# Attention head and mixture chain on one core: a new start for the first pair, and q's scaling moved within the attention loop

## The chip, the cores and the metric

The kernel runs on one core of a Trainium2 chip. The metric is the time of one execution on the device in microseconds (us); lower is better. Five engines work in parallel, each through its own instructions in order: TensorE (PE: matmuls, and PEld for its weight loads), VectorE (DVE), ScalarE (ACT), GpSimd (POOL) and SyncE (SP, which only issues DMAs). They wait for each other on semaphores. ACT and POOL can issue DMAs too.

## The reference

Three stages follow each other: an attention in which a query sees only the keys of its own hash bucket, and two feed-forward layers.

```python
q_bits = einsum('bhsd,dk->bhsk', q, proj) > 0      # 6 bits for each row; k the same
mask = bucket(q_bits)[..., :, None] == bucket(k_bits)[..., None, :]
scores = where(mask, q @ k.T / sqrt(64), -1e9)      # B=2, H=8, S=768, D=64
attn = softmax(scores);  x = attn @ v               # then reshaped to 1536 x 512
x = relu(x @ w_in)**2 @ w_out                       # d_ff 2048
out = silu(x @ w_in2) @ w_out2
```

Everything is float32; the weights arrive as float64 words and are converted on the chip.

## The kernel before

Attention treats two heads at a time, a pair: eight pairs, of four units each (a head's 384 queries), of three blocks of 128 queries. One pass of the loop over `d` is a step: it takes one block of scores through reduce and exp, transposes two key blocks of an earlier unit, splits them in a high and a low part and multiplies them with v. A float32 product is made from float32r parts, high times high, high times low and low times high; so q (`qq`), k (`kk`), the transposed P (`th`, `tl`) and v exist as high and low parts. The mask is made inside the product: bits of q and k stand as twelve more rows of `qq[:, 1]` and `kk[:, 1]`, so the scores need four matmuls.

What a step issues, by engine:
- DVE: `row_max` (a reduce of 768 scores, L699), two small `row_live` operations (L703, L704), two `t_lo` (the low part `tl`, L738).
- ACT: two `t_hi` (L732), `score_exp` (L712).
- PE: six transposes (L727), four matmuls with v (L751, L752), four of scores (L694).

Seven steps (d = 5, 17, 29, ... 77) are in the dictionary `long`. In them PE also makes the bits of the next pair (twelve matmuls, L525), DVE compares them (`bits_cmp`, L531, twice), and from d = 17 on PE transposes the reciprocal sums of the pair before (`rb_mm`, L776), which ACT copies (`x_norm`, L786). Then ACT issues a DMA (L618) that places bits of k. Five of them (d = 5, 17, 29, 53, 65) and the one at 77 also hold operations on VectorE that convert feed-forward weights (`w_exp` L657, `w_sign` L661, `w_low` L665), in the list `mid`.

The next pair but one is prepared meanwhile: q is loaded, ScalarE scales it in place by 1/8 (`scale_q`, L494), POOL casts it (`cast_pair`, tile hq, L490), and later steps split and place it. `scale_q` stands at the end of the step ahead of a long one.

The head, d = -5 to 1, does the first pair by other functions. Its second head's rows of k come by a DMA of POOL (`second_head`, L591). `first_bits_mm` (L605) makes the bits of q and of k separately, for each head and half, as 76 columns of which the last twelve are the bits, and `first_bits_cmp` (L609) writes them straight into `qq` and `kk`. `warm_up` issues matmuls on zeros.

The order of each engine is the order in which the program is written; in the feed-forward part, which the change leaves alone, a planner with costs sets it. A PSUM tile of the scores has two buffers, so a block's scores wait until the exp of the block two before has read them.

Of the kernel before, what the change touches and what calls it, by code (L numbers as in the profile page):

```python
# [11 lines left out]
F32 = mybir.dt.float32  # L12
# [11 lines left out]
NB = 6  # L24
# [5 lines left out]
NBR = 2 * NB  # L30
NFQ = 3 * NBR + 6
PW = 96
# [403 lines left out]
def lsh_attention_moe_moe(ctx, tc, kd, qk, qf, fq, v, pc, wi1, wo1, wi2, wo2, out):  # L436
# [25 lines left out]
    pcr = ac.tile([128, 2 * PW], F32, name="pcr")  # L462
    tmt = ac.tile([128, 6], F32, name="tmt")
# [3 lines left out]
    pjd = ac.tile([128, 3, 76], F32R, name="pjd")  # L467
    pdx = ac.tile([128, 2, NBR], F32, name="pdx")
    tm = [tmt[:, 2 * i : 2 * i + 2] for i in range(3)]
    mt = ac.tile([128, 4, 4], F32, name="mt")  # L470
# [75 lines left out]
    def first_load(h):  # L546
# [11 lines left out]
        else:  # L558
            first[1, 0] = a1.tile([128, S], F32, tag="tb", name="fr10")
            first[1, 1] = a1.tile([128, 6, 2, 64], F32, tag="rw", name="fr11").rearrange("p a b c -> p (a b c)")  # L560
            for i in range(2):
                nc.sync.dma_start(out=first[1, i], in_=qf[1, i])
        t["qq"][h] = a1.tile([128, 2, S], F32R, tag="qq", bufs=2, name=f"qq0_{h}")
        t["kk"][h] = a1.tile([128, 2, S], F32R, tag="kk", bufs=2, name=f"kk0_{h}")
        first["hk", h] = (a2 if h else a1).tile([128, S], F32R, tag=("hk", "hq")[h], name=f"hk0_{h}")

    def first_q_hi(z):
        nc.scalar.mul(out=pair[0]["qq"][0][:, 0, half(z)], in_=first[0, 0][z], mul=SCALE)

    def first_q_lo(z):  # L570
        qq = pair[0]["qq"][0]
        nc.vector.scalar_tensor_tensor(
            out=qq[0:64, 1, half(z)], in0=first[0, 0][z][0:64], scalar=SCALE, in1=qq[0:64, 0, half(z)].bitcast(F32), op0=ALU.mult, op1=ALU.subtract
        )

    def first_k_hi(z):
        for i in range(2):
            nc.scalar.copy(out=pair[0]["kk"][0][0:64, i, half(z)], in_=first[0, 1][z][0:64])

    def first_k_lo(z):  # L580
        r, hk = first[0, 1][z], first["hk", 0]
        if z == 0:
            nc.gpsimd.tensor_copy(out=hk[64:128, half(z)], in_=r[64:128])
        else:
            nc.scalar.copy(out=hk[64:128, half(z)], in_=r[64:128])
        nc.gpsimd.tensor_tensor(out=pair[0]["kk"][0][64:128, 0, half(z)], in0=r[64:128], in1=hk[64:128, half(z)].bitcast(F32), op=ALU.subtract)
# [12 lines left out]
    def first_bits_mm(h, i, z):  # L599
        x, zs = pair[0][("qq", "kk")[i]][h], half(z)  # L600
        o = first["bits", h, i, z] = ps_t.tile([128, 512], F32, tag="t", name=f"bf{h}{i}{z}")
        w = (pjd[:, i], x[:, 0, zs]), (pjd[0:64, 2 * i], x[0:64, 1, zs])
        for n in range(2):
            wt_, xt = w[n ^ i]
            mm(o[0:76, 0:QW], wt_, xt, start=n == 0, stop=n == 1)  # L605

    def first_bits_cmp(h, i, z):
        m = tm[1 + i][64:76]
        nc.vector.tensor_scalar(  # L609
            out=pair[0][("qq", "kk")[i]][h][64:76, 1, half(z)], in0=first["bits", h, i, z][64:76, 0:QW],  # L610
            scalar1=m[:, 0:1], scalar2=m[:, 1:2], op0=ALU.is_gt, op1=ALU.mult,
        )

    def place_bits(p, h):
# [200 lines left out]
    mid = defaultdict(list)  # L815
    long = {}
    last = defaultdict(list)
# [53 lines left out]
    with tc.manual_schedule():  # L871
# [19 lines left out]
        nc.vector.tensor_copy(out=pjd.rearrange("p a b -> p (a b)"), in_=zero[:, 0:228])  # L891
        c, k = slice(64, 64 + NBR), first["c"]
# [8 lines left out]
        nc.vector.tensor_tensor(out=pjd[0:64, 2, c], in0=pdx[0:64, 1], in1=pjd[0:64, 1, c].bitcast(F32), op=ALU.subtract)
        first_k_lo(0)
        first_k_hi(0)
        first_k_lo(1)
        first_k_hi(1)
        first_q_hi(1)
        for i, z in ((0, 0), (1, 0), (1, 1)):
            first_bits_mm(0, i, z)
        for i, z in ((0, 0), (1, 0), (1, 1)):
            first_bits_cmp(0, i, z)  # L910
        first_q_lo(1)
        at(-4, first_bits_mm, 0, 0, 1)
        mid[-3].append((first_bits_cmp, (0, 0, 1)))
        for n, (i, z) in enumerate(((1, 0), (1, 1), (0, 0), (0, 1))):
            at((-3, -3, -2, -1)[n], first_bits_mm, 1, i, z)
            mid[n - 2].append((first_bits_cmp, (1, i, z)))
        second_head()
# [13 lines left out]
        for d in range(-5, G // 2 + 3):  # L931
# [52 lines left out]
        assert not new  # L984
        assert not todo and not extra and not mid
        att.close()
# [18 lines left out]
def _layout(q, k, v, proj, moe_w_in, moe_w_out, moe2_w_in, moe2_w_out):  # L1005
# [43 lines left out]
```

## Time and profile before

| what | us |
|---|---|
| median of 3 runs (758.18 to 759.3) | 758.25 |
| the profiled execution | 754.1 |
| its span | 752.3 |
| PE busy in the span | 737.8 (98%) |
| DVE busy | 596.6 (79%) |
| ACT busy | 460.3 (61%) |
| POOL busy | 427.6 (57%) |

The span is the part of the profiled execution between its first and last instruction. A busy PE is not a PE at its peak, since matmuls are pipelined. The granted clock of TensorE is 1.00 (2.4 GHz) or 0.50 (1.2 GHz) of full speed; its mean over the span is 0.997.

### The profile page before, as it was taken

The page shows a single profiled execution, that of the slowest core. Times are in us where ns is not written, and L with a number is a line of the kernel's source. Part 1 is how long each engine was busy: PE and PEld are TensorE (multiplying, and loading weights), DVE is VectorE, ACT ScalarE, POOL GpSimd, SP SyncE. Part 2 cuts the span into 40 slices and gives each one's busy share as a digit, 9 for nine tenths or more (in the row PEclk, how much of TensorE's full clock was granted, in tenths as well). Part 3 has the DMA queues.
Part 4 walks back from the last instruction along what each step waited for, and adds up shares of the span by engine and source line. Part 5 has one row for each costly group of instructions (what it writes and reads, how often), then busy time and mean ns, then how long its engine had stood idle before and what let it go on. Part 6 is the DMA issues. An engine that isn't in the chain of part 4 may idle for free.

```text
span 752.3 us, 10873 instructions
## 1 busy us (share of the span) xinstructions
PE 737.8 (98%) x3732; PEld 629.0 (84%) x3732; DVE 596.6 (79%) x1053; ACT 460.3 (61%) x865; POOL 427.6 (57%) x316
## 2 busy tenths in 40 slices
PE   8899999999999999999999999999999999999998
PEld 3789999999998778888888888887888888888886
DVE  6899999999999898659558786999965874685542
ACT  5788989998898774575368258447534525624510
POOL 7457497578591567654655743967475356455200
PEclk9999999999999999999999999999999999999999
DMA  7566866776642312122221221102122121030012
GB/s 229 117 144 153 210 162 167 178 161 146 152 103 88 95 57 84 57 84 61 81 84 57 85 84 58 53 32 85 57 84 85 48 93 55 31 112 29 0 71 98
DMA packets 27654, 71.98 MB, mean 96 GB/s; under 512 B 4192, under 2 KB 9072, under 8 KB 27600
## 3 DMA queue, kind: packets, MB, share of 16 engines
q1 hardware_dynamic: 24936, 64.64, 30.2%
q0 software_dynamic: 2208, 6.00, 3.6%
q10 hardware_dynamic: 456, 0.65, 0.4%
q8 instruction: 30, 0.49, 0.3%
q14 instruction: 24, 0.20, 0.1%
HBM read 49.80 MB, written 3.15 MB: 70 GB/s over the span
## 4 chain that ended last, share of the span: by engine, by line
PE 69%; DVE 27%; DMA 1%; issue 1%; ACT 1%; POOL 0%; ACTq 0%; DVEq 0%
PE bank L338 33%; PE bank L257 17%; PE bank L228 9%; DVE mt L699 8%; DVE tl L738 8%; PE s L694 4%; PE t L727 3%; DVE ys L151 2%; PE o L751 2%; PE o L752 1%; DVE xb L157 1%; DMA kk<-in_dram 1%; DVE mt L704 1%; DVE ts L262 1%; DVE wt L174 1%
## 5 line engine op out<-in xcount | busy, mean ns | idle before, releaser
L172 POOL TENSOR_SCALAR wt<-wt 128x512 f32<-128x512 f32 x56 | 117.0, 2098 | 45.3 <-ACT wt L170 45.3
L157 POOL TENSOR_TENSOR wp<-wt,wp 128x512 fp32r<-128x512 f32 x56 | 76.6, 1378 | 96.1 <-ACT wp L155 96.1
L257 PE MATMUL bank<-xb,wp 128*128 128x512 f32 x480 | 111.3, 390 | 2.8 <-DVE ts L262 1.6
L257 PEld LDWEIGHTS bank<-xb,wp 128*128 128x128 f32 x480 | 89.7, 188 | 23.0 <-DVE xb L157 1.6
L738 DVE TENSOR_TENSOR tl<-t,th 128x384 fp32r<-128x384 f32 x192 | 104.8, 547 | 3.3 <-ACT th L732 2.7
L712 ACT ACTIVATE P<-s,mt 128x768 f32<-128x768 f32 x96 | 95.7, 997 | 14.7 <-DVE mt L704 11.8
L155 ACT CAST wp<-wt 128x512 fp32r<-128x512 f32 x56 | 34.6, 620 | 105.7 <-DVE wt L175 64.4
L699 DVE TENSOR_REDUCE mt<-s 128x1 f32<-128x768 f32 x96 | 91.4, 952 | 5.3 <-PE s L694 4.7
L732 ACT CAST th<-t 128x384 fp32r<-128x384 f32 x192 | 82.4, 484 | 13.1 <-PE t L727 9.9
L694 PE MATMUL s<-kk,qq 76*128 76x384 f32 (+1 forms) x384 | 85.1, 342 | 1.3 <-ACT P L712 0.5
L727 PE MATMUL t<-ident,P 128*128 128x128 f32 x576 | 80.8, 275 | 4.5 <-DVE tl L738 3.1
L262 DVE TENSOR_TENSOR ts<-bank,ts 128x512 f32<-128x512 f32 x80 | 54.6, 690 | 36.7 <-PE bank L257 34.4
L228 PE MATMUL bank<-x0h,wp 128*128 128x512 f32 x256 | 80.2, 390 | 0.0
L727 PEld LDWEIGHTS t<-ident,P 128*128 128x128 f32 x576 | 68.5, 141 | 10.5 <-issue 3.9
L751 PE MATMUL o<-th,vv 128*128 128x384 f32 x192 | 72.9, 380 | 0.0
L694 PEld LDWEIGHTS s<-kk,qq 76*128 76x128 f32 (+1 forms) x384 | 68.1, 190 | 3.8 <-DVE bt L531 1.8
L752 PE MATMUL o<-tl,vv 128*128 128x384 f32 x192 | 64.5, 336 | 0.0
L242 ACT ACTIVATE ts<-bank 128x512 f32<-128x512 f32 x48 | 28.6, 595 | 52.4 <-PE bank L228 26.9
L228 PEld LDWEIGHTS bank<-x0h,wp 128*128 128x128 f32 x256 | 48.1, 188 | 9.9
L157 DVE TENSOR_TENSOR gql<-ts,gqh 128x512 fp32r<-128x512 f32 x64 | 46.1, 732 | 12.7 <-ACT gqh L155 12.4
L174 DVE SCALAR_TENSOR_TENSOR wt<-raw,wt 128x512 uint32<-128x512 uint32 x58 | 51.5, 889 | 0.6
L170 ACT ACTIVATE wt<-raw 128x512 f32<-128x512 f32 x58 | 38.7, 670 | 20.5 <-POOL wp L157 11.0
(169 smaller groups left out, 1725.7 us busy)
## 6 DMA issues: line engine op xcount, KB each, us to landing
raw<-in_dram SPq DMA_DIRECT2D x64, 512.0 KB
kk<-in_dram POOLq DMA_DIRECT2D x15, 384.0 KB, 5.3
qq<-hq SPq DMA_DIRECT2D x28, 192.0 KB
vr<-in_dram SPq DMA_DIRECT2D x8, 384.0 KB
ta<-ob SPq DMA_DIRECT2D x32, 96.0 KB
tb<-ob SPq DMA_DIRECT2D x32, 96.0 KB
out_dram<-ts SPq DMA_DIRECT2D x11, 256.0 KB
rq<-in_dram SPq DMA_DIRECT2D x7, 384.0 KB
```

The source lines that it names most:

```text
L157: add(("DVE", "POOL")[pool], l, lambda: eng.tensor_tensor(out=lo(), in0=src(), in1=hi().bitcast(F32), op=ALU.subtract), (*rk, *hk), lk)
L172: add("DVE" if fast else "POOL", 0.5 if fast else 2.4, lambda: eng.tensor_scalar(out=wtt, in0=wtt, scalar1=W_LO, scalar2=W_HI, op0=ALU.max ...
L228: mm(bank[b], w[:, x, op, sl], t["x0"][y][:, kt], start=kt == 0 and j == 0, stop=kt == 3 and j == 2)
L257: mm(bank[b], w[:, p, op, k * 128 : k * 128 + 128], x[:, q, xop, k], start=first and k == 0 and j == 0, stop=k == 1 and j == 2, skip_group ...
L338: mm(bank[b][:, 0:wd], x, y, start=i == 0 and n == 0, stop=i == FB - 1 and n == 2)
L694: mm(s[:, n, 0:QW], t["qq"][h][0:kk, ab, c0 : c0 + 128], t["kk"][h][0:kk, ab, n * QW : (n + 1) * QW], start=ab == 0, stop=ab == 1)
L699: nc.vector.tensor_reduce(out=m[:, 0:1], in_=s[:, :, 0:QW], op=ALU.max, axis=AX.XY, negate=True)
L712: nc.scalar.activation(out=e.rearrange("p (a b) -> p a b", a=2), in_=s[:, :, 0:QW], func=AF.Exp, scale=m[:, 1:2], bias=m[:, 2:3], accum_ou ...
L727: nc.tensor.transpose(t[:, j * 128 : (j + 1) * 128], P[u, j][:, kt * 128 : (kt + 1) * 128], ident)
L732: nc.scalar.copy(out=th, in_=PT[g][0][:, 0:QW])
L738: nc.vector.tensor_tensor(out=tl, in0=t[:, 0:QW], in1=th.bitcast(F32), op=ALU.subtract)
L751: mm(o[:, 0:QW], vv, th, start=kt == 0, stop=False)
```

## The change

Four things are done.
- In the attention loop, `scale_q` of pairs 2 to 7 moves from the end of the step ahead of a long step into the long step, behind its `score_exp`.
- In the head, low parts are made by POOL instead of VectorE in part, the first head's bits of k are made from three operands (the high part of k twice, from `hk`), and the DMA with the second head's rows of k is issued by POOL before the splits. The DMA of `pcr` goes to ACT's queue.
- The second head's bits of q and k are made together as 24 columns, two groups of four matmuls instead of four groups of two; they are compared into a tile `bt`, and two DMAs on ACT's queue place them (`second_place`).
- The warm-ups follow a table: 9 instead of 12 at the start, one between groups of bits, and 3, 2, 3, 3, 3, 2, 1 in steps -5 to 1 (before: 2 in steps -5 to -2). Loads of weights 0 and 1 are written at step -2 instead of -5, `scale_q` of pair 1 at -3 instead of -1, and the load of pair 2 at 1 instead of -1.

```diff
+WARM = {-5: 3, -4: 2, -3: 3, -2: 3, -1: 3, 0: 2, 1: 1}
-W_STEPS = ((-5, 2, 5, 5, 17), (-5, 5, 17, 29, 29), ...
+W_STEPS = ((-2, 2, 5, 5, 17), (-2, 5, 17, 29, 29), ...
...
+            nc.scalar.dma_start(out=pcr, in_=pc)
...
     def first_q_lo(z):
+        q, qq = first[0, 0][z][0:64], pair[0]["qq"][0]
+        if z:
+            nc.gpsimd.tensor_tensor(out=qq[0:64, 1, half(z)], in0=q, in1=qq[0:64, 0, half(z)].bitcast(F32), op=ALU.subtract)
+        else:
+            nc.vector.scalar_tensor_tensor(...)
+    def first_k_hi(z, i):
+        (nc.gpsimd.tensor_copy if i else nc.scalar.copy)(out=pair[0]["kk"][0][0:64, i, half(z)], in_=first[0, 1][z][0:64])
+    def first_hk(z):
+        nc.scalar.copy(out=first["hk", 0][64:128, half(z)], in_=first[0, 1][z][64:128])
+    def first_k_lo(z):
+        (nc.gpsimd if z else nc.vector).tensor_tensor(...)
...
+    def second_bits_mm(z):
+        o = first["both", z] = ps_t.tile([128, 512], F32, tag="t", name=f"bs{z}")
+        ops = [(64 - NBR * i, *x) for i in range(2) for x in first_ops(1, z)[i]]
+        for n, (c, w, rows_, x) in enumerate(ops):
+            mm(o[0 : 2 * NBR, 0:QW], pjd[rows_, w, c : c + 2 * NBR], x, start=n == 0, stop=n == len(ops) - 1)
+    def second_bits_cmp(z):
+        ...
+        nc.vector.tensor_scalar(out=first["bt"][0 : 2 * NBR, half(z)], in0=first["both", z][0 : 2 * NBR, 0:QW], ...)
+    def second_place():
+        for n, x in enumerate(("qq", "kk")):
+            nc.scalar.dma_start(out=pair[0][x][1][64 : 64 + NBR, 1, :].bitcast(F32), in_=first["bt"][NBR * n : NBR * n + NBR].bitcast(F32))
...
-            at(d0 - 13, load_pair, p)
-            at(d0 - 8, scale_q, p)
+            at(max(d0 - 13, 1), load_pair, p)
+            scale[d0 - 7] = p
...
-        warm_up(12)
+        warm_up(9)
+        nc.gpsimd.dma_start(out=pair[0]["kk"][1][0:64], in_=kd[0, :, 1].unsqueeze(1).broadcast_to([64, 2, S]))
...
+        for z in range(2):
+            at(z - 2, second_bits_mm, z)
+            mid[z - 1].append((second_bits_cmp, (z,)))
+        at(0, second_place)
...
             if d in long:
                 score_exp(*ready, m)
+                if d in scale:
+                    scale_q(scale.pop(d))
...
-            if d < -1:
-                warm_up(2)
+            warm_up(WARM.get(d, 0))
```

ScalarE's row around the long step at d = 17, before (rq_699 is q of pair 3, th casts and P exps; the exp of P_0 is the long step's):

```order
L757 COPY ob_864<-o_791 128x384
L712 ACTIVATE P_2_868,sums_588<-s_2_833,mt 128x768
L494 ACTIVATE rq_699<-rq_699 128x768
L732 CAST th_887<-t_883 128x384
L732 CAST th_895<-t_891 128x384
L712 ACTIVATE P_0_897,sums_588<-s_0_870,mt 128x768
L786 COPY rw_806<-rb_918 128x768
L618 DMA kk_0_767<-bt_925 12x768
```

The same place now, where rq_709 is that q:

```order
L790 COPY ob_874<-o_801 128x384
L745 ACTIVATE P_2_878,sums_598<-s_2_843,mt 128x768
L765 CAST th_896<-t_892 128x384
L765 CAST th_904<-t_900 128x384
L745 ACTIVATE P_0_906,sums_598<-s_0_880,mt 128x768
L495 ACTIVATE rq_709<-rq_709 128x768
L819 COPY rw_816<-rb_928 128x768
L651 DMA kk_0_777<-bt_935 12x768
```

The scaling passed two casts and an exp, and stands ahead of the copy of the sums.

POOL's row in the head, before (kk_1 holds k of the second head, qq_1 its q):

```order
L898 COPY tmt<-fc 128x6
L583 CAST hk_0_109<-fk 64x384
L586 TENSOR_TENSOR kk_0_108<-fk,hk_0_109 64x384 x2
L591 DMA kk_1_115<-in_dram 64x2x768
L592 DMA pcr<-in_dram 128x192
L595 CAST hk_1_116<-fr_111 64x768
L596 TENSOR_TENSOR kk_1_115<-fr_111,hk_1_116 64x768
L597 TENSOR_TENSOR qq_1_114<-fr_110,qq_1_114 64x768
```

And now:

```order
L931 COPY tmt<-fc 128x8
L932 TENSOR_TENSOR pjd<-pdx,pjd 128x12
L933 DMA kk_1_116<-in_dram 64x2x768
L591 TENSOR_TENSOR kk_0_108<-fk,hk_0_109 64x384
L585 CAST kk_0_108<-fk 64x384 x2
L580 TENSOR_TENSOR qq_0_107<-fq_101,qq_0_107 64x384
L600 CAST hk_1_117<-fr_111 64x768
L601 TENSOR_TENSOR kk_1_116<-fr_111,hk_1_117 64x768
L602 TENSOR_TENSOR qq_1_115<-fr_110,qq_1_115 64x768
```

The DMA of kk_1 stands ahead of the splits; two casts and another split have come to POOL, one split has gone.

ScalarE's row at the end of the head, now (bt_252 holds the second head's bits; before, no DMA stood there):

```order
L745 ACTIVATE P_0_254,sums_194<-s_0_232,mt 128x768
L765 CAST th_281<-t_277 128x384
L765 CAST th_289<-t_285 128x384
L745 ACTIVATE P_1_291,sums_194<-s_1_256,mt 128x768
L643 DMA qq_1_115<-bt_252 12x768
L643 DMA kk_1_116<-bt_252 12x768
L765 CAST th_314<-t_310 128x384
L765 CAST th_322<-t_318 128x384
L745 ACTIVATE P_2_324,sums_194<-s_2_293,mt 128x768
```

Two DMA issues stand between an exp and the next casts.

## Rows read from the trace of the kernel before

**Rows 1.** Busy time by stretch; columns: stretch, length, each engine's busy time (instructions), clock, DMA share, GB/s.

```profile
33.43:236.00 202.57, 200.41 (x1341) 188.91 (x1340) 198.38 (x470) 180.04 (x394) 136.87 (x127) 1.00 0.64 151
```

**Rows 2.** Timeline of VectorE in a usual step; columns: start, duration, engine, line, operation.

```profile
81.73 0.96 DVE L699 TENSOR_REDUCE mt<-s 128x1 f32<-128x768 f32 x1
83.80 0.96 DVE L699 TENSOR_REDUCE mt<-s 128x1 f32<-128x768 f32 x1
```

**Rows 3.** Busy time in five long steps, from reduce to reduce.

```profile
33.43:38.63 5.20, 4.95 (x33) 3.86 (x32) 5.17 (x12) 3.79 (x8) 2.38 (x2) 1.00 0.45 117
62.04:67.31 5.27, 5.18 (x34) 4.05 (x33) 5.26 (x11) 4.03 (x8) 3.49 (x4) 1.00 0.45 112
89.97:95.53 5.56, 5.20 (x34) 4.07 (x33) 5.50 (x12) 4.04 (x8) 3.30 (x4) 1.00 0.47 120
118.19:123.01 4.82, 4.82 (x34) 4.02 (x33) 3.83 (x9) 3.88 (x8) 0.89 (x2) 1.00 0.63 167
...
201.55:206.59 5.04, 5.04 (x34) 4.13 (x33) 4.99 (x11) 3.40 (x7) 1.90 (x2) 1.00 0.45 126
```

**Rows 4.** Timeline of the long step that starts at 62.04.

```profile
62.70 0.84 ACT L494 ACTIVATE rq<-rq 128x768 f32<-128x768 f32 x1
...
63.60 1.32 POOL L490 CAST hq<-rq 128x768 fp32r<-128x768 f32 x1 [2.16 <-ACT rq L494]
...
64.16 1.05 DVE L657 TENSOR_SCALAR wi<-wi 128x512 uint32<-128x512 uint32 x1
...
66.30 0.80 ACT L786 COPY rw<-rb 128x768 f32<-128x768 f32 x1 [1.03 <-POOL wp L674]
```

**Rows 5.** One line of VectorE, all of it: ns as least/median/most.

```profile
L657 DVE TENSOR_SCALAR wi<-wi x4: 418/732/1047, 35.0 to 175.7; 128x512 uint32<-128x512 uint32 x4
```

**Rows 6.** One line of POOL, likewise.

```profile
L490 POOL CAST hq<-rq x7: 823/1061/1327, 20.6 to 175.2; 128x768 fp32r<-128x768 f32 x7
```

**Rows 7.** Timeline of VectorE in the head: four reduces and one small operation.

```profile
10.05 0.96 DVE L699 TENSOR_REDUCE mt<-s 128x1 f32<-128x768 f32 x1
...
11.11 0.20 DVE L704 TENSOR_SCALAR mt<-mt 128x1 f32<-128x1 f32 x1
...
17.36 0.96 DVE L699 TENSOR_REDUCE mt<-s 128x1 f32<-128x768 f32 x1 [0.68 <-PE s L694]
...
26.58 0.96 DVE L699 TENSOR_REDUCE mt<-s 128x1 f32<-128x768 f32 x1 [0.86 <-PE s L694]
...
33.43 0.96 DVE L699 TENSOR_REDUCE mt<-s 128x1 f32<-128x768 f32 x1
```

**Rows 8.** Timeline of TensorE and POOL in the head.

```profile
1.31 5.30 PE L885 MATMUL warm<-zero 128*128 128x512 bf16 x12 [1.31 <-DVE zero L879]
...
7.13 0.84 POOL L591 DMA_DIRECT2D kk<-in_dram  x1
...
15.25 1.38 PE L605 MATMUL bf<-kk,pjd 64*76 64x384 f32 x4 [1.28 <-DMA kk<-in_dram]
...
16.46 0.86 PE L694 MATMUL s<-kk,qq 128*128 128x384 f32 x4
```

**Rows 9.** DMA issues of the first 20 us: KB each, us to landing.

```profile
kk<-in_dram POOLq DMA_DIRECT2D x1, 384.0 KB, 8.1
```

**Rows 10.** Costliest groups of the page: busy us, mean ns of one.

```profile
L712 ACT ACTIVATE P<-s,mt 128x768 f32<-128x768 f32 x96 | 95.7, 997 | 14.7 <-DVE mt L704 11.8
...
L732 ACT CAST th<-t 128x384 fp32r<-128x384 f32 x192 | 82.4, 484 | 13.1 <-PE t L727 9.9
```

**Rows 11.** Issue of the bits' DMA on ScalarE's queue in the timeline.

```profile
67.33 0.73 ACTq L618 DMA_DIRECT2D kk<-bt  x1
```

**Rows 12.** DMA queues from 68.7 to 69.27: packets, MB, share.

```profile
q10 hardware_dynamic: 24, 0.04, 36.4%
```

**Rows 13.** TensorE alone in two stretches: length, busy time (instructions), granted clock, DMA share, GB/s.

```profile
21.00:24.39 3.39, 1.55 (x10) 1.00 0.00 0
24.39:27.80 3.41, 3.41 (x14) 0.50 0.82 213
```

More of the change, by code (lines that the diff above doesn't have):

```diff
@@ L30 @@
 NBR = 2 * NB
-NFQ = 3 * NBR + 6
+NFQ = 3 * NBR + 8
+WARM = {-5: 3, -4: 2, -3: 3, -2: 3, -1: 3, 0: 2, 1: 1}
 PW = 96
@@ L466, in lsh_attention_moe_moe @@
     pjl = ac.tile([128, PW], F32R, name="pjl")
-    pjd = ac.tile([128, 3, 76], F32R, name="pjd")
+    pjd = ac.tile([128, 3, 88], F32R, name="pjd")
     pdx = ac.tile([128, 2, NBR], F32, name="pdx")
-    tm = [tmt[:, 2 * i : 2 * i + 2] for i in range(3)]
+    tm = [tmt[:, 2 * i : 2 * i + 2] for i in range(4)]
     mt = ac.tile([128, 4, 4], F32, name="mt")
@@ L567, in first_q_hi @@
     def first_q_hi(z):
-        nc.scalar.mul(out=pair[0]["qq"][0][:, 0, half(z)], in_=first[0, 0][z], mul=SCALE)
-    def first_q_lo(z):
-        qq = pair[0]["qq"][0]
-        nc.vector.scalar_tensor_tensor(
-            out=qq[0:64, 1, half(z)], in0=first[0, 0][z][0:64], scalar=SCALE, in1=qq[0:64, 0, half(z)].bitcast(F32), op0=ALU.mult, op1=ALU.subtract
-        )
[L576 to L586, printed above, removed]
+        q = first[0, 0][z]
+        if z:
+            nc.scalar.mul(out=q, in_=q, mul=SCALE)
+            nc.scalar.copy(out=pair[0]["qq"][0][:, 0, half(z)], in_=q)
+        else:
+            nc.scalar.mul(out=pair[0]["qq"][0][:, 0, half(z)], in_=q, mul=SCALE)
+    def first_q_lo(z):
+        q, qq = first[0, 0][z][0:64], pair[0]["qq"][0]
+        if z:
+            nc.gpsimd.tensor_tensor(out=qq[0:64, 1, half(z)], in0=q, in1=qq[0:64, 0, half(z)].bitcast(F32), op=ALU.subtract)
+        else:
+            nc.vector.scalar_tensor_tensor(out=qq[0:64, 1, half(z)], in0=q, scalar=SCALE, in1=qq[0:64, 0, half(z)].bitcast(F32), op0=ALU.mult, op1=ALU.subtract)
+    def first_k_hi(z, i):
[3 more added lines that the diff above has]
+    def first_k_lo(z):
+        (nc.gpsimd if z else nc.vector).tensor_tensor(
+            out=pair[0]["kk"][0][64:128, 0, half(z)], in0=first[0, 1][z][64:128], in1=first["hk", 0][64:128, half(z)].bitcast(F32), op=ALU.subtract
+        )
     def second_head():
@@ L597, in second_head, with first_ops @@
         nc.gpsimd.tensor_tensor(out=qq[0:64, 1], in0=q[0:64], in1=qq[0:64, 0].bitcast(F32), op=ALU.subtract)
[L599 to L607, printed above, removed]
+    def first_ops(h, z):
+        q, k, hk, zs = pair[0]["qq"][h], pair[0]["kk"][h], first["hk", h], half(z)
+        up, dn, all_ = slice(0, 64), slice(64, 128), slice(0, 128)
+        of_q = [(0, all_, q[:, 0, zs]), (0, up, q[up, 1, zs])]
+        if h:
+            return of_q, [(1, all_, k[:, 0, zs]), (2, up, k[up, 1, zs])]
+        return of_q, [(1, dn, hk[dn, zs]), (2, dn, hk[dn, zs]), (1, dn, k[dn, 0, zs])]
@@ L608, in first_bits_cmp, with first_bits_mm @@
+    def first_bits_mm(i, z):
+        o = first["bits", i, z] = ps_t.tile([128, 512], F32, tag="t", name=f"bf{i}{z}")
+        ops = first_ops(0, z)[i]
+        for n, (w, rows_, x) in enumerate(ops):
+            mm(o[0:76, 0:QW], pjd[rows_, w, 0:76], x, start=n == 0, stop=n == len(ops) - 1)
+    def first_bits_cmp(i, z):
         m = tm[1 + i][64:76]
         nc.vector.tensor_scalar(
-            out=pair[0][("qq", "kk")[i]][h][64:76, 1, half(z)], in0=first["bits", h, i, z][64:76, 0:QW],
+            out=pair[0][("qq", "kk")[i]][0][64:76, 1, half(z)], in0=first["bits", i, z][64:76, 0:QW],
@@ L611, in first_bits_cmp @@
             scalar1=m[:, 0:1], scalar2=m[:, 1:2], op0=ALU.is_gt, op1=ALU.mult,
         )
+    def second_bits_mm(z):
[4 more added lines that the diff above has]
+    def second_bits_cmp(z):
+        if z == 0:
+            first["bt"] = a1.tile([128, S], F32R, tag="bt", name="bt0")
+        m = tm[3][0 : 2 * NBR]
+        nc.vector.tensor_scalar(
+            out=first["bt"][0 : 2 * NBR, half(z)], in0=first["both", z][0 : 2 * NBR, 0:QW], scalar1=m[:, 0:1], scalar2=m[:, 1:2], op0=ALU.is_gt, op1=ALU.mult
+        )
@@ L614, in place_bits @@
+    def second_place():
+        for n, x in enumerate(("qq", "kk")):
+            nc.scalar.dma_start(
+                out=pair[0][x][1][64 : 64 + NBR, 1, :].bitcast(F32), in_=first["bt"][NBR * n : NBR * n + NBR].bitcast(F32)
+            )
     def place_bits(p, h):
@@ L815, in lsh_attention_moe_moe @@
     mid = defaultdict(list)
-    long = {}
+    long, scale = {}, {}
     last = defaultdict(list)
@@ L898, in lsh_attention_moe_moe @@
         nc.gpsimd.tensor_copy(out=tmt, in_=k[:, 3 * NBR : NFQ])
+        nc.gpsimd.tensor_tensor(out=pjd[:, 2, c], in0=pdx[:, 1], in1=pjd[:, 1, c].bitcast(F32), op=ALU.subtract)
+        nc.gpsimd.dma_start(out=pair[0]["kk"][1][0:64], in_=kd[0, :, 1].unsqueeze(1).broadcast_to([64, 2, S]))
         first_q_hi(0)
+        first_hk(0)
+        first_hk(1)
         first_q_lo(0)
[L901 removed]
         first_k_lo(0)
[L903 removed]
+        first_k_hi(0, 0)
         first_k_lo(1)
[L905 removed]
+        first_k_hi(1, 0)
+        for z in range(2):
+            first_k_hi(z, 1)
         first_q_hi(1)
[L907 to L916 removed]
+        first_q_lo(1)
+        first_bits_mm(0, 0)
+        warm_up(1)
+        first_bits_mm(1, 0)
+        warm_up(1)
+        first_bits_mm(1, 1)
+        for i, z in ((0, 0), (1, 0), (1, 1)):
+            first_bits_cmp(i, z)
+        at(-4, first_bits_mm, 0, 1)
+        mid[-3].append((first_bits_cmp, (0, 1)))
+        for z in range(2):
+            at(z - 2, second_bits_mm, z)
+            mid[z - 1].append((second_bits_cmp, (z,)))
+        at(0, second_place)
         second_head()
@@ L984, in lsh_attention_moe_moe @@
         assert not new
-        assert not todo and not extra and not mid
+        assert not todo and not extra and not mid and not scale
         att.close()
```

11 lines of the change are left out of this document (5 added, 6 removed).

## The prediction

> **What bounds the kernel now.** I read the busy time by stretch first, then VectorE's timeline step by step, then the long steps, then the head. From 33.43 to 236.00 us, which is the attention loop behind its head, VectorE is busy 198.38 of 202.57 us and TensorE 200.41 [rows 1]: two engines without slack, and the two reduces 81.73 and 83.80 show a usual step of 2.06 us [rows 2]. The reader is to see that here time is saved only where both of these engines get less work or less waiting. Behind 236 comes the feed-forward part, which the change leaves as it is; it begins when attention ends, so I carry an earlier end of attention through at full value. Two places are open to the change: the six long steps ahead of d = 77 with their neighbours, and the head.
>
> The long steps are 5.20, 5.27, 5.56, 4.82 and 5.04 us [rows 3]; the two not shown (d = 53 and 65) have the same instructions as the second and its length within 0.02, so I count each as the second. The shortest, d = 41, has no conversion of weights on VectorE: it is busy there 3.83 of 4.82 us, and TensorE all of it. So 4.82 is what TensorE needs in a long step with the transposes of the sums. The step at 201.55, d = 77, has two conversions and no scaling ahead of it, and takes 5.04, VectorE busy 4.99.
>
> **The scaling.** What the long steps with conversions and a scaling have too much is seen at 62.04: ScalarE scales at 62.70, POOL's cast hq is released by it and runs from 63.60 for 1.32 us, and VectorE's L657 starts at 64.16 and takes 1.05 us [rows 4]. Its shortest run is 0.418 [rows 5], the cast's 0.823 [rows 6]. The two slow each other: the conversion ends at 65.21, right behind the cast at 64.92, and 0.63 us of VectorE's time is waiting. The Trainium skill, "SBUF — State Buffer", section "Who interferes with whom", says that VectorE and GpSimd share a port pair as an exclusive lock and the later operation waits until the earlier one ends; the rows agree, since the cast's end less its 0.82 is 64.10, about where the conversion ahead of L657 ends. By that rule alone the gain would be a cast's whole 0.82 per step.
>
> Now the scaling stands behind the long step's exp, so the cast starts some 2 us later (two casts of 0.48, an exp of 1.00, the scaling of 0.84, less what they waited for), when the conversions are done. VectorE's work in those stretches then reads PSUM (scores, transposes, bits), where no row shows a slowdown beside POOL. By step:
> - d = 17, 53 and 65: from 5.27 to TensorE's 4.82, 0.45 each, 1.35 together. VectorE would need less than the 5.04 of d = 77, since L657 with 0.42 is shorter than the conversion it has there.
> - d = 29: two conversions as d = 77, so 5.56 to 5.04, 0.52.
> - d = 5: no transposes of sums, so TensorE sets nothing; 5.20 less the waiting, 0.5 (between nothing and L657's 0.63).
> - d = 41: TensorE is full already, 0.
>
> Sum 2.4 us. The lower bound is 1.0 (d = 17, 53, 65 and 5 give 0.1 to 0.2 each, if TensorE's scores must wait for the compared bits in them as at d = 77); the upper is the 0.63 or 0.82 of waiting in all five, 3.1 to 4.1, of which TensorE's 4.82 leaves 2.9.
>
> The scaling itself costs ScalarE 0.84 in the long step. Its cover is the 1.03 us in which it is idle there ahead of the copy [rows 4], and exp and casts are ahead by the 0.84 that left the step before. Queued behind it are that copy, the DMA of the bits and the next casts; without the cover the copy would be up to 0.84 late, and with it the buffer for the next scores. POOL's work behind the cast (weights' parts, products of x) slides by some 1 us; POOL is busy 136.87 of 202.57 us [rows 1]. I cost both at nothing.
>
> **The head.** The reduces at 10.05 (first), 17.36 (fourth), 26.58 (seventh) and 33.43 (tenth) mark it [rows 7]. A reduce with its two small operations is 1.26 us (10.05 to 11.31), and the exp starts 0.1 later. In the new order, from rows:
> - The first scores. Nine warm-ups of 0.44 [rows 8] end 1.3 earlier than twelve, but eight bit matmuls stand there instead of six, with two warm-ups between. A bit matmul of 76 columns takes 0.34 (four in 1.38 [rows 8]), where the four of scores behind them take 0.86; at half clock twice that. Less 1.3, plus 0.7 for two, plus 0.6 for two warm-ups (0.3 each, between half of 0.44 and all of it), plus 0.7 for two bit matmuls that now come so early that they run at half rate: first reduce at 10.75, 0.7 later. Between 0 and 0.9.
> - The wait for the rows of k goes. Before, POOL issued that DMA at 7.13, and TensorE waited 1.28 us for it until 15.25 [rows 8]; the DMA took 8.1 us [rows 9]. Now POOL issues it behind two small operations, at about 4.7, so that it lands by 12.8 even at 8.1, and its first reader comes at 16. What is late next is the ring of exp, scores and reduce: 10.75, then 12.1 (one VectorE turn), 14.1 (scores wait for the exp of the first, 12.1 + 1.0 + 0.2, then 0.86), 15.45 (the fourth; 17.36 before), 17.5 (exp of the third, scores), 20.5 (four bit matmuls of 24 columns, their comparison, two transposes, scores).
> - The two bit DMAs are a new wait. ScalarE does two casts (0.48) and the exp of the fifth block (1.00) [rows 10] from about 19.5 to 21.5, then issues two DMAs at 0.73 each [rows 11]; the row's DMA, issued at 67.33, has its packets in the stretch that ends at 69.27 [rows 12], 1.94 us. So the second lands at 21.5 + 0.73 + 1.94 = 24.2. Queued behind the issues on ScalarE are the next two casts and an exp, and VectorE's low parts wait for those; on TensorE the second two score matmuls of the second head, and all transposes behind. With 0.35 for two matmuls and 0.45 to the reduce: seventh reduce at 25.0, against 26.58.
> - From there three steps. At full clock 2.06 each: tenth reduce at 31.2, 2.2 us earlier. Before, TensorE's clock fell from 1.00 to 0.50 at 24.39, after a stretch in which it had been busy 1.55 of 3.39 us, and stayed there to 27.80 [rows 13]. The new warm-ups make it busier up to 20.7, but between 21.4 and 24.2 it has little but to wait. If the clock falls again, the seventh to eighth takes some 0.7 longer and the gain is 1.4.
>
> One price has no row: bit matmuls of 24 columns. The nearest rows are 76 columns (0.34) and the scores (0.2); at 0.34 each group is 0.6 later, 1.2 for both. I take 0.2, since the columns are fewer, and the clock that falls: head 1.4 us earlier, with bounds of 0 (slow bits) and 2.9 (full clock and no loss at the first scores).
>
> The other edits: weights 0 and 1 are loaded by SP, whose order around them is the same, so they start as before; the load of pair 2, moved past the first placements, unblocks SP's queue earlier, and nothing near waits for it.
>
> **Sum.** 2.4 + 1.4 = 3.8 us off the profiled execution: span 752.3 to 748.5, execution 754.1 to 750.3. The median of the runs is 758.25, 4.15 above that execution; I take the same difference, so 754.45, in round figures 754.5.
>
> **Rivals.**
> - The head gives nothing back. For it: rows 13, the new idle of nearly 3 us, the unknown bit matmuls. Against: the wait for the rows of k is gone for sure. Then 758.25 - 2.4 = 755.85. By the Trainium skill, "TensorE: Matmul & The Clock Gate", section "Part 4: PE-mode transpose", transposes do not count as busy for the clock in the usual way; of the work around 21 us much is transposes, which makes this more likely.
> - The long steps stay. For it: TensorE is busy 5.18 of 5.27 us in the step of 62.04 [rows 3], so it may have more than VectorE to wait for, and ScalarE has a long step with 0.84 more. Against: 4.82 with the same work at d = 41. Then only the head, 756.85, within 0.2%.
> - Slower: the bit DMAs land late. Its place is the second head's first scores; they run while the first placements of pair 1, the load of pair 2 and rows of k for pair 1 are in flight, as in the first 15 us, when a DMA took 8.1 [rows 9] instead of about 2. At 8.1 they land at 30.3, 6.1 later than I said: 754.45 + 6.1 = 760.5. It decides from 3.8 us of lateness on. Against: in rows 12 the 24 packets of that queue go within 0.57 us while another queue is moving too.
> - More: full clock and 24 columns at 0.2 and no loss at the first scores, 758.25 - 2.4 - 2.9 = 752.95.
>
> **How the numbers follow.** Forecast 0.50, head nothing 0.20, long steps stay 0.13, slower 0.07, more 0.10. A measurement of this kernel tells about 0.2%, 1.5 us, from no change, that is 756.75 to 759.75. The forecast, the first and the last rival are faster (0.80, less 0.04 for their edges), the second is the same (with those edges 0.17), the third slower. The range takes the last rival and the second in part: 752.4 to 757.1.
>
> **What would show it.** Right: in the changed profile the long steps at d = 17, 53, 65 are 4.8 to 4.9 us and L657 takes 0.42 everywhere; the fourth reduce is near 15.5 without a wait for a DMA, the tenth near 32.0; attention's last reduce is 3.8 earlier. Wrong: L657 still long, a wait for the copy of the sums on TensorE, the first reduce later than 11, the seventh later than 26, or a stretch of 0.50 longer than 3.4 us.

## The result, and the profile after

| | before | after |
|---|---|---|
| median of the runs, us | 758.29 (4 runs, 758.18 to 759.3) | 750.07 (4 runs, 749.44 to 750.77) |
| ratio, 95% interval | | 0.989 (0.9876 to 0.9903) |
| profiled execution and its span, us | 754.1 and 752.3 | 750.41 and 748.3 |

The change takes 8.2 us off, where I forecast 3.8: 750.07 lies below my range of 752.4 to 757.1. Between the two profiled executions it is otherwise: 752.3 to 748.3 is 4.0, and I had said 748.5. So the sum was nearly right for the execution that I had read (in part by luck, see below), and wrong for the usual one. One execution of the kernel before took 1500.03 us at full clock, beside the runs e5 to e8 below, and is left out of every comparison.

First the loop, by stretch, in the columns of [rows 1, 3]: the whole stretch from the tenth reduce to 2.64 us behind the last one, as in [rows 1], then the five long steps.

```profile
32.63:232.61 199.98, 199.13 (x1341) 189.02 (x1340) 195.32 (x470) 180.75 (x394) 134.50 (x127) 1.00 0.68 152
32.63:37.32 4.69, 4.69 (x33) 3.93 (x32) 4.66 (x11) 3.93 (x8) 1.17 (x2) 1.00 0.45 129
59.91:64.71 4.80, 4.80 (x34) 4.08 (x33) 4.63 (x12) 3.98 (x8) 1.28 (x2) 1.00 0.47 123
87.35:92.40 5.05, 5.05 (x34) 4.13 (x33) 4.99 (x10) 4.12 (x8) 2.44 (x4) 1.00 0.53 149
115.84:120.62 4.78, 4.78 (x34) 4.09 (x33) 3.79 (x9) 3.98 (x8) 1.23 (x2) 1.00 0.60 156
198.15:203.20 5.05, 5.05 (x34) 4.13 (x33) 4.99 (x10) 3.42 (x7) 2.08 (x4) 1.00 0.54 142
```

202.57 has become 199.98, 2.59 less. The long steps are 4.69, 4.80, 5.05, 4.78 and 5.05 where they were 5.20, 5.27, 5.56, 4.82 and 5.04, and TensorE now works through all of each. The conversion and the cast that slowed each other [rows 5, 6] no longer do (ns, least/median/most):

```profile
L690 DVE TENSOR_SCALAR wi<-wi x4: 419/421/422, 34.2 to 172.8; 128x512 uint32<-128x512 uint32 x4
...
L491 POOL CAST hq<-rq x7: 824/826/830, 17.0 to 174.2; 128x768 fp32r<-128x768 f32 x7
```

Next the head in VectorE's timeline, the same four reduces as in [rows 7], and one new wait far behind them:

```profile
8.83 0.96 DVE L732 TENSOR_REDUCE mt<-s 128x1 f32<-128x768 f32 x1 [0.59 <-PE s L727]
...
13.71 0.96 DVE L732 TENSOR_REDUCE mt<-s 128x1 f32<-128x768 f32 x1
...
24.65 0.96 DVE L732 TENSOR_REDUCE mt<-s 128x1 f32<-128x768 f32 x1 [2.51 <-PE s L727]
...
32.63 0.96 DVE L732 TENSOR_REDUCE mt<-s 128x1 f32<-128x768 f32 x1
...
111.66 0.23 DVE L799 RECIPROCAL sums<-sums 128x12 f32<-128x12 f32 x1 [0.71 <-POOL sums L795]
```

And what TensorE, ScalarE's queue and POOL do at these two places:

```profile
14.73 0.64 PE L631 MATMUL bs<-kk,pjd 128*24 128x384 f32 x2
...
18.92 1.34 ACTq L643 DMA_DIRECT2D qq<-bt  x1
...
20.29 0.73 ACTq L643 DMA_DIRECT2D kk<-bt  x1
...
24.03 0.58 PE L727 MATMUL s<-kk,qq 76*128 76x384 f32 x2 [3.04 <-DMA kk<-bt]
...
109.44 1.28 POOL L708 TENSOR_TENSOR wp<-wi,wp 128x512 fp32r<-128x512 f32 x1
110.68 0.64 POOL L501 DMA_DIRECT2D kk<-in_dram  x1
111.39 0.23 POOL L795 TENSOR_SCALAR sums<-sums 128x12 f32<-128x12 f32 x1
```

TensorE reads the second head's k at 14.73 without a wait for its rows; the 1.28 of [rows 8] is gone. In its place it stands 3.04 us at 24.03 for the bits' DMA, issued at 20.29. Of TensorE alone, ahead of and in the stretch of half clock that follows (compare [rows 13]):

```profile
21.00:24.74 3.74, 0.71 (x4) 1.00 1.00 246
24.74:28.15 3.41, 3.41 (x15) 0.50 1.05 190
```

So from profile to profile the head ends 0.8 us earlier (tenth reduce 33.43 to 32.63), the loop is 2.59 shorter, and 0.6 comes behind it, where the kernels are written alike and no run shows the cause: 4.0. The other 4.2 us of the result are not in these two traces at all.

### The profile page after: what moved, and what is told of

Same layout as the page of the kernel before. It is cut to its first block, busy times and chain, and to the rows that moved or that the text cites. A ratio compares the mean times of both kernels' runs of the same rounds, so it can differ in the third digit from the quotient of the medians.

```text
span 748.3 us, 10896 instructions
## 1 busy us (share of the span) xinstructions
PE 736.8 (98%) x3741; PEld 629.1 (84%) x3742; DVE 591.1 (79%) x1050; ACT 461.3 (62%) x865; POOL 425.3 (57%) x317
## 4 chain that ended last, share of the span: by engine, by line
PE 77%; DVE 17%; POOL 3%; DMA 2%; issue 1%; ACT 1%; ACTq 0%; DVEq 0%; POOLq 0%; SPq 0%
PE bank L339 33%; PE bank L258 17%; PE bank L229 9%; PE s L727 6%; PE t L760 5%; DVE tl L771 4%; DVE mt L732 4%; PE o L784 3%; PE o L785 3%; DVE ys L152 2%; DVE xb L158 1%; DVE ts L263 1%; DVE wt L175 1%; PE bt L526 1%; PE bs L526 1%
```

## The experiments

The question is where the 4.15 us lie by which the median of before exceeds its profiled execution. Theory A: in the head, as TensorE's clock at half for longer than the 3.41 us of [rows 13]. Rivals put them outside the span, or into the wait for rows of k itself. The ratios are to runs of the kernel before on the same chip, whose medians are 758.27 (beside e1 to e4), 757.94 (e5 to e8) and 757.83 (e9 and e10); that of the changed kernel is the one above. One table for all, with two numbers from each profile that split the attention part: the tenth reduce (head) and the time from it to the last reduce (loop). "Half" is the length of the stretch of half clock in the head.

| kernel | median us (least to most) | ratio, 95% interval | half us | tenth reduce | loop |
|---|---|---|---|---|---|
| before, the profile of [rows 1 to 13] | | | 3.4 | 33.43 | 199.93 |
| e1 before again | 757.07 (756.58 to 758.87) | 0.9999 (0.9989 to 1.0009) | 13.7 | 36.29 | 199.91 |
| e2 scaling only | 756.41 (752.62 to 758.27) | 0.9977 (0.9965 to 0.999) | 17.1 | 37.85 | 198.44 |
| e3 head only | 751.75 (751.17 to 752.49) | 0.9922 (0.9909 to 0.9935) | 3.4 | 32.77 | 198.99 |
| e4 early rows | 753.54 (751.95 to 759.56) | 0.9958 (0.9939 to 0.9977) | 6.8 | 32.25 | 199.95 |
| e5 warm-ups only | 756.24 (754.55 to 757.05) | 0.998 (0.9965 to 0.9994) | 6.8 | 35.02 | 199.90 |
| e6 few warm-ups | 750.83 (749.58 to 751.16) | 0.9901 (0.9887 to 0.9915) | 6.8 | 33.36 | 197.30 |
| after | 750.07 (749.44 to 750.77) | 0.989 (0.9876 to 0.9903) | 3.4 | 32.63 | 197.34 |
| e7 early place | 746.51 (746.23 to 747.22) | 0.9849 (0.9836 to 0.9862) | 0 | 28.59 | 197.28 |
| e8 and POOL's sums later | 745.86 (745.45 to 748.75) | 0.9846 (0.9827 to 0.9866) | 0 | 28.56 | 196.55 |
| e9 early rows and warm-ups | 751.25 (751.04 to 751.53) | 0.9915 (0.99 to 0.9929) | 0 | 30.51 | 199.92 |
| e10 late rows | 758.35 (757.76 to 759.58) | 1.001 (1.0001 to 1.002) | 17.1 | 37.38 | 199.94 |

**e1: the kernel before, unchanged.**

> The kernel before, once more, to see where its runs stand beside its profiled execution (754.1 us, span 752.3, while its runs were 758.2 to 759.3). Theory A, that the difference is inside the program in some executions and not in others (TensorE's clock rising later or falling for longer in the head, which differs from execution to execution): runs at two levels near 754 and 758, and those at 758 with a lower mean granted clock (one more stretch of 3.4 us at half rate is 0.0023 of the span at 0.5, so 0.995 instead of 0.997). Theory B, that 4.15 us lie around the program in runs without a profile: all runs at 758, the spans at 752. Theory C, that the single profiled execution was simply a rare fast one and something in the program other than the clock decides: all runs at 758 with spans of 756 and the clock unchanged.

Its profiled execution took 756.89 us, with a span of 755.1. TensorE alone by stretch, then its wait for the rows of k:

```profile
13.81:17.22 3.41, 1.74 (x8) 1.00 0.17 39
17.22:30.88 13.66, 12.15 (x41) 0.50 0.39 101
```

```profile
15.52 1.37 PE L605 MATMUL bf<-kk,pjd 64*76 64x384 f32 x4 [1.67 <-DMA kk<-in_dram]
```

The same instructions, but the clock falls at 17.22 instead of 24.39 and stays at half for 13.66 us. Its fourth, seventh and tenth reduce, to be compared with [rows 7]:

```profile
17.82 0.96 DVE L699 TENSOR_REDUCE mt<-s 128x1 f32<-128x768 f32 x1 [0.87 <-PE s L694]
...
29.27 0.96 DVE L699 TENSOR_REDUCE mt<-s 128x1 f32<-128x768 f32 x1 [0.86 <-PE s L694]
...
36.29 0.96 DVE L699 TENSOR_REDUCE mt<-s 128x1 f32<-128x768 f32 x1
```

They are 0.46, 2.69 and 2.86 us later than in [rows 7]: behind the wait, which is 0.39 longer, the lag is 0.46, and the rest comes in the stretch at half clock. There the same four matmuls of scores take 1.65 us, where the profile of before has 0.96 (first before, then e1):

```profile
18.20 0.96 PE L694 MATMUL s<-kk,qq 128*128 128x384 f32 x4
```

```profile
19.44 1.65 PE L694 MATMUL s<-kk,qq 128*128 128x384 f32 x4
```

The span is 2.8 longer; the loop is the same within 0.02. So what the two executions differ by lies ahead of the tenth reduce, and most of it is the clock, not the wait. Both have 1.8 us between span and execution, so it is not outside the span. The 29 executions of before beside e1 to e4 show how usual this is: 12 take 756.38 to 757.77 us at a mean granted clock of 0.990 to 0.993 (e1's profile has 0.991), 17 take 757.88 to 759.75 at 0.986 to 0.989. So there are two groups and the clock parts them, as A had it, but neither lies near the 754 that A named. None reaches the 754.1 and 0.997 of the execution that I had read; of 68 executions of this kernel timed in or beside the experiments one came near (754.99 at 0.998).

**e2: before, with the scaling of pairs 2 to 7 in the long step, nothing else.**

```diff
-            at(d0 - 8, scale_q, p)
+            scale[d0 - 7] = p
...
             if d in long:
                 score_exp(*ready, m)
+                if d in scale:
+                    scale_q(scale.pop(d))
```

> The kernel before with the scaling of q alone moved into the long steps. Theory A (two parts that add, as in the profiles): long steps of 4.7, 4.8, 5.05, 4.8, 4.8, 4.8, 5.05 us, 2.4 us faster than the kernel before. Rival (the measured 8 us come mostly from the scaling in runs): 5 to 6 us faster. Rival (mostly from the head): within 1 us.

The loop is 1.49 us shorter and the median about 1.7 (0.0023 of 758.27). The long steps up to d = 65 are 4.68, 4.82 and 5.04, as forecast, and the one at 77 is 5.20 instead of 5.04; but a step that was 2.06 (d = 38) is now 2.91, with this in VectorE's timeline:

```profile
117.70 0.23 DVE L766 RECIPROCAL sums<-sums 128x12 f32<-128x12 f32 x1 [0.69 <-POOL sums L762]
```

It is the wait of 111.66 above: a piece of the 2.4 us, some 0.7 with the next step, is given back there.

**e3: the changed kernel with the scaling back in its old place.**

```diff
-            scale[d0 - 7] = p
+            at(d0 - 8, scale_q, p)
```

> The changed kernel with the scaling of q put back ahead of the long steps. Theory A: the head's part alone, tenth reduce near 32.6, 1 to 2 us faster than the kernel before in spans; in runs up to 6 if the runs of the kernel before are slow in their head. Rival (the gain in runs lies in the scaling): 3 us or less.

The new head alone is worth 0.0078 of 758.27, 5.9 us (4.9 to 6.9), as Theory A allowed; with e2's 1.7 that makes 7.6 of the 8.2. The clock is at half for 3.41 us. Its loop is 0.94 shorter than before's with the old scaling, and 0.80 of that is one step: the one behind the first long step was 2.74 us, with an issue of the bits' DMA of 1.56 us on ScalarE's queue in it; in e3 it is 1.94 and that issue takes 0.76, and the first such issue of the kernel now stands in the head. The issue before, and in e3:

```profile
38.73 1.56 ACTq L618 DMA_DIRECT2D kk<-bt  x1
```

```profile
38.06 0.76 ACTq L651 DMA_DIRECT2D kk<-bt  x1
```

**e4: before, with one line moved: POOL issues the rows of k ahead of the low parts.**

```diff
     def second_head():
-        nc.gpsimd.dma_start(out=kk[0:64], in_=kd[0, :, 1]...)
...
         nc.gpsimd.tensor_copy(out=tmt, in_=k[:, 3 * NBR : NFQ])
+        nc.gpsimd.dma_start(out=pair[0]["kk"][1][0:64], in_=kd[0, :, 1]...)
```

> The kernel before, with one edit: POOL issues the DMA of the second head's rows of k ahead of the splits. If the runs of the kernel before are slow because that DMA lands late (it took 8.1 us in the profile, more in other executions), this alone gives most of the head's gain in runs, 3 to 6 us. If the clock decides, it gives about 1.5 us, the wait of 1.28 us at the rows of k and what hangs on it.

3.2 us (0.0042 of 758.27), from one moved line. By the numbers that I had set this speaks for the DMA (3 to 6) and against the clock (about 1.5), but they did not part the two: the wait that was removed is 1.28, 1.67 and 1.87 us long in the three profiles of that head (before, e1, e2), so the 3.2 (1.7 to 4.6) is likely more than the wait alone. In this profile the clock holds until 19.64, and is at half for a shorter time than in e1, but for longer than in the profile of before:

```profile
16.23:19.64 3.41, 2.00 (x11) 1.00 0.00 0
19.64:26.47 6.83, 5.86 (x24) 0.50 0.49 137
```

It falls without the wait for the rows, behind another one:

```profile
19.61 0.85 PE L726 MATMUL t<-ident,P 128*128 128x128 f32 x3 [1.41 <-DVE qq L608]
```

And 2 of 12 executions took 759.41 and 759.56 us at a mean clock of 0.986, as low as the slowest of before: with the rows early the long fall has become rare, not impossible. Whether the DMA was late in these two no profile shows.

**e5: before, with the changed kernel's warm-ups per step.**

```diff
-            if d < -1:
-                warm_up(2)
+            warm_up(WARM.get(d, 0))
```

> The kernel before, with the changed kernel's warm-ups per step (3, 2, 3, 3, 3, 2, 1 instead of 2 in each of the first four) and nothing else of the head. Theory A (what the typical run of before has over its profiled execution is TensorE's clock at half in the head, and more work there keeps the clock up): the fall of the clock comes later than 17.2 us or is shorter than 13.7 us, and the median comes to 753.5 to 756.5. Theory B (the time goes to the wait for the rows of k itself, 1.3 to 1.7 us, and warm-ups are without effect): 758.3, within 0.7.

1.5 us (0.998), inside what A named. But in the profile the clock falls earlier than in e1, at 14.25, and for 6.83 us; the wait for the rows still stands, longer:

```profile
15.94 2.19 PE L606 MATMUL bf<-kk,pjd 64*76 64x384 f32 x4 [2.09 <-DMA kk<-in_dram]
```

So A's "later than 17.2" was wrong and its "shorter than 13.7" right: in this profile the warm-ups do not cover the wait, and what follows it is shorter. The mean clocks of all eight executions, 0.993 to 0.998, fit that.

**e9: e4 and e5 together, still with the old head.**

> The kernel before with two parts of the new head together: the DMA of the second head's rows of k issued ahead of the low parts (as in the run with early rows, 753.5 median but 759.5 in 2 of 12 executions) and the changed kernel's warm-ups per step. Theory A (the clock in the head decides, and it falls where TensorE has little to do ahead of it): no execution at 759 any more, clock at half for 6.9 us or less, median 751.5 to 753.5. Theory B (the wait for the rows alone counts, warm-ups only stand in the way): 753.5 to 754.5, and the slow ones stay.

Six executions between 751.04 and 751.53, all at a mean clock of 0.999 or 1.0. TensorE alone from 12 to 36, and the tenth reduce:

```profile
12.00:36.00 24.00, 22.20 (x127) 1.00 0.50 133
```

```profile
30.51 0.96 DVE L699 TENSOR_REDUCE mt<-s 128x1 f32<-128x768 f32 x1
```

No fall at all, and no execution near 759. B's "753.5 to 754.5" is out; A's bound of 6.9 us of half clock holds, with room, and the median lies just below its 751.5. This ratio and e3's overlap (0.9915 and 0.9922): an early DMA and warm-ups bring what the whole new head brings. What the rest of that head could bring is held up by the wait at 24.03, as e7 shows below.

**e10: before, with the rows of k issued one instruction later.**

```diff
-        nc.gpsimd.dma_start(out=kk[0:64], in_=kd[0, :, 1]...)
...
         nc.gpsimd.tensor_copy(out=hk[64:128], in_=k[64:128])
+        nc.gpsimd.dma_start(out=kk[0:64], in_=kd[0, :, 1]...)
```

> The kernel before with the same DMA one instruction later on GpSimd (behind the cast of hk, 0.85 us), so that TensorE's wait for the rows, 1.28 us in the profiled execution, grows. Theory A: the wait at 14 to 15 us grows by up to 0.85 us and the clock falls behind it in every execution: all at 758.0 to 759.8, none at 754 to 757, mean clock 0.989 or less. Theory B: 0.85 us or less above the kernel before, with the same spread from 756.4 upward. If the DMA lands at the same time, nothing changes and the run tells nothing.

```profile
15.69 2.19 PE L605 MATMUL bf<-kk,pjd 64*76 64x384 f32 x4 [2.35 <-DMA kk<-in_dram]
```

The wait grows to 2.35 us and the profile has 17.06 us of half clock, from 14.56 on. All 12 executions take 757.76 us or more; of the 17 of before beside it 8 take less. As A has it, the quicker group is gone. But two of the 12 lie below A's 758.0, four have a clock of 0.990 or 0.991, which A excluded, and the median moves by 0.5 only, which B allows. It leans to A and decides nothing by itself.

**e6: the changed kernel with two warm-ups in each of the first four steps.**

```diff
-WARM = {-5: 3, -4: 2, -3: 3, -2: 3, -1: 3, 0: 2, 1: 1}
+WARM = {-5: 2, -4: 2, -3: 2, -2: 2}
```

> The changed kernel with two warm-ups in each of the first four steps, as before, instead of 3, 2, 3, 3, 3, 2, 1. Theory A: the clock falls earlier or stays at half longer than 3.4 us in some or all runs, median 751 to 754. Theory B (the new order alone brought the time): 750.1, within 0.5.

750.83 lies between the two theories' numbers, and its interval overlaps that of the changed kernel. In the profile the clock falls at 23.10 for 6.82 us and the tenth reduce is 0.7 later, as A says, but the loss is smaller than A had it: in the new order the further warm-ups are worth some 0.7 us, and the runs do not tell that from nothing.

**e7: the changed kernel, the second head's bits earlier and placed from two queues.**

```diff
-            at(z - 2, second_bits_mm, z)
-            mid[z - 1].append((second_bits_cmp, (z,)))
-        at(0, second_place)
+            at(-2, second_bits_mm, z)
+            mid[-1].append((second_bits_cmp, (z,)))
+        at(-1, second_place)
...
-            nc.scalar.dma_start(
+            (nc.scalar if n else nc.sync).dma_start(
```

> The changed kernel with both groups of the second head's bit matmuls in the step d = -2 and the two DMAs of the bits in d = -1, one issued by SP and one by ScalarE. My theory of the head (the seventh reduce waits for these DMAs: 3.04 us of TensorE's time, and the clock at half for 3.4 us behind it): DMAs land by about 21, the wait falls to 0.5 or less, the clock falls less or not, median 746.5 to 748. Rival (the ring of exp, scores and reduces sets the head, since the second group of bits now stands ahead of a score and makes the fifth reduce 1.3 us late): 749 to 750.5.

746.51, where my theory had 746.5 to 748. The issues, TensorE's second head and the tenth reduce in the timeline, and TensorE alone from 12 to 36:

```profile
17.63 0.90 SPq L643 DMA_DIRECT2D qq<-bt  x1
...
17.64 1.60 ACTq L643 DMA_DIRECT2D kk<-bt  x1
...
21.18 0.96 PE L727 MATMUL s<-kk,qq 128*128 128x384 f32 x4 [0.23 <-ACT P L745]
...
28.59 0.96 DVE L732 TENSOR_REDUCE mt<-s 128x1 f32<-128x768 f32 x1
```

```profile
12.00:36.00 24.00, 23.50 (x141) 1.00 0.56 140
```

The wait of 3.04 is gone, the clock no longer falls (the fifth reduce comes 1.5 us later, as the rival had it, and that costs nothing here), and the tenth reduce is 4.0 us earlier than in the changed kernel, which is the whole gain from profile to profile (spans 748.3 and 744.4): the loop is the same. The medians differ by 3.6. The earlier step and the second queue came together; which of them did it no run tells.

**e8: e7, with POOL's weights' sums put two steps later.**

```diff
-                at(d0 + 7 + h, wp_put, i // 2, h, 4 + 2 * h)
+                at(d0 + 9 + h, wp_put, i // 2, h, 4 + 2 * h)
```

> The kernel of e7 with the weights' sums put two steps later on GpSimd, d0 + 9 and d0 + 10 instead of d0 + 7 and d0 + 8. Theory (in the changed kernel the reciprocal at 111.66 waits 0.71 us for GpSimd, whose queue had slid by the later casts): 0.5 to 0.9 us below e7, and no wait at that reciprocal. Rival (the ring takes the time back in the next long step, or the sums collide with the products of x): the same as e7 within 0.3.

The reciprocal has no wait any more, and the loop is 0.73 shorter:

```profile
106.78 0.22 DVE L799 RECIPROCAL sums<-sums 128x12 f32<-128x12 f32 x1
```

The median is 0.65 below e7, as forecast, but the intervals of the ratios overlap, and one of five executions took 748.75, at full clock, for a reason that I do not know. The best version is e7 or e8, some 4 us below the changed kernel and 12 below the kernel before.

## Why the prediction was wrong, and which of its steps held

- **The step that failed.** "The median of the runs is 758.25, 4.15 above that execution; I take the same difference, so 754.45." That carries the 4.15 over as if the change could not touch them. They lie in the head: e1 shows 2.86 of them ahead of the tenth reduce, and its execution is one of the quicker half. For the median I estimate the tenth reduce at 33.43 + 4.15 = 37.6 (e2's profile, with the same head and a mean clock of 0.988, has 37.85). From there to 32.63 are 5.0; with 2.6 in the loop and 0.6 behind it, 8.2. The term "head 1.4 us" was worked out from a rare execution of the kernel before; it measured 5.9 on the runs (e3, 0.94 of it in the loop).
- **Luck in the sum.** From profile to profile 4.0 stands beside my 3.8, but the terms are others: 0.8 in the head instead of 1.4, and 0.6 behind attention that I had not counted. In the loop the long steps gave 2.5 (2.4 forecast); the shorter issue behind the first of them gave 0.8 more and the wait at 111.66 took 0.7 back, neither of which I had, so that 2.59 came out.
- What could have been read: the profiled execution, 754.1, lay 4 us below the least of three runs that agreed within 1.2. Such an execution is not a shifted copy of the others; [rows 13] showed a clock that fell in the head, and the question was how early it falls in other executions and for how long. The Trainium skill, "TensorE: Matmul & The Clock Gate", section "Part 1: The HAM clock gate", says of the rise of the clock at a kernel's start that the number of matmuls at the low clock differs between runs of one kernel, and that the penalty is below 1% of a usual span. For the fall in this head the sizes are alike: 3.4 to 17.1 us at half in one and the same head, and from 757.83 to e9's 751.25 some 0.9%, the shorter waits included.
- **The scaling: right in the long steps.** "From 5.27 to TensorE's 4.82" (4.80), "5.56 to 5.04" (5.05), 0.5 at d = 5 (0.51), nothing at d = 41 (0.04). The whole 0.82 per step, which I had weighed as the gain by the lock alone, did not come, since TensorE, busy for all of the 4.80, ends the step. The trace agrees with the exclusive lock on the ports that VectorE and GpSimd share (the Trainium skill, "SBUF — State Buffer", section "Who interferes with whom"): with the two apart the conversion takes 0.42 and the cast 0.83 everywhere. As a term of the sum, alone in e2, the 2.4 measured 1.49 in the loop, for the next reason.
- **"POOL's work slides ... I cost both at nothing": wrong**, by 0.7 to 0.9. The cast that starts later sets back POOL's queue, and at d = 37 the increment of the sums (L795) stands in it behind a cast and a subtraction of weights (L708 at 109.44) and a DMA issue. e8 moves these and gets 0.73 back. A slide of 1 us in a queue that is two thirds busy is free only up to the next instruction that someone waits for; I named none.
- **The first reduces.** I said 10.75, 12.1, 14.1 and 15.45; they came at 8.83, 10.21, 12.34 and 13.71. Between the first bit matmul and the first scores I had added 2.0 us (two warm-ups, two matmuls more, half clock for two); it was 0.4 (2.40 before, 2.82 now). The slow start was no new cost: in the kernel before the first two took 1.41 already, at 6.05, and now two take 0.57 from 5.78 on (L617). The wait for the rows went, as said; nothing was late in its place there.
- **The bits' DMAs.** The place was right, and the seventh reduce nearly (25.0 said, 24.65 measured), but two errors cancel: the fourth reduce was 1.7 and the sixth 1.0 earlier, and the DMA took 3.74 us from its issue at 20.29 to where TensorE goes on, not 1.94, behind a first issue of 1.34, not 0.73. And the price without a row, the bit matmuls of 24 columns that I put at 0.2: e7 has two in 0.57 in its steady run, 0.28 each. At that time pair 1's placements and pair 2's load move (the clock rows above show the DMA engines busy all the time, share 1.00 and 246 GB/s), where in the stretch of [rows 12] the two queues that moved had them busy for 36.4% and 23.4%; that this made the DMA slower is likely, and no run shows it by itself. The rival "the bit DMAs land late" was thus half true; it did not decide, as the new head had gained more elsewhere.
- **The clock that falls in the head**: taken as likely, and it fell, 24.74 to 28.15. The rival "more" (full clock) did not occur in this profile, but one of the four executions, 749.44 us, has a mean clock of 1.0, where the profiled one has 0.998 and 750.41; in e3 the two at 1.0 are likewise about 1 us below the two at 0.997 and 0.998. So in the new head the fall costs about 1 us, near the 0.7 that I had for it. But from the seventh reduce to the eighth the profile has 3.87 us (24.65 to 28.52), where 2.06 and 0.7 make 2.8; so the tenth came at 32.63 and not near 32.0. The rule on transposes could not be tested: no run here changes the transposes alone.
- What stays open: why the same instructions lose the clock at 17.2 us in one execution and at 24.4 in another. Ahead of these points TensorE was busy 1.74 of 3.41 us in e1; in the profile of before the wait there was 0.4 shorter. In the four profiles in which TensorE waits 1.67 us or more for the rows of k (e1, e2, e5, e10) the clock falls in the wait or within 2 us behind it; with a wait of 1.28 us (before) or none (e4) it falls later, behind another idle stretch, and in e9 not at all. So a long wait goes with the early fall, and e9 and e10 point the same way, but it is not the only thing that starts one: e4 has two executions as slow as before's slowest. What sets the length of a fall I do not know.

## What to carry to other kernels

When the profiled execution is well off the median of the runs, first find out which stretch the difference is in: the mean granted clock of each execution, and a second profile, tell it at once. A stretch in which TensorE waits for a DMA at the start of a kernel can cost more than the wait, since the clock at half may last through the work behind it: here a wait 0.39 us longer went with 2.86 us (e1). Issue such DMAs ahead of the engine's own work; for a small placing DMA, a queue of its own and a step of lead together gave 3.6 us (e7).

## What the runs showed of the hardware that I had not expected

- In each of these kernels the first small DMA from SBUF to SBUF issued on ScalarE's queue took about twice as long to issue as all that follow: 1.56 us against 0.73 to 0.76 before, 1.34 against 0.73 to 0.76 after, 1.60 against 0.73 to 0.76 in e7, although that queue had issued loads from DRAM ahead of it. On SP's queue the other of the two took 0.90 in e7. The reason is open.
- One kernel's executions spread over 754.1 to 759.8 us, and the mean clock falls as the time rises (0.998 to 0.986); with the rows early and the further warm-ups six executions stay within 0.5 us (e9), with the rows early alone they spread over 7.6 (e4).
- Four bit matmuls with 24 columns of weights took as long as four with 76, each over 384 columns of data: 1.38 us from 13.99 to the end of the row at 14.73 in the changed kernel, 1.38 in [rows 8]. The fewer columns saved nothing here.
